# Moving loads, small row transfers and one group of products inside a gated linear attention step that runs ahead of a mixture-of-experts layer

## The chip, the cores and the metric

The kernel runs on one core of a Trainium2 chip. The core has a tensor engine (TensorE, PE in the profile), a vector engine (VectorE, DVE), a scalar engine (ScalarE, ACT), a general engine (GpSimd, POOL) and a sync engine (SyncE, SP) that here only issues transfers. Each engine works through its own instructions in order and waits on semaphores for the others. Transfers are issued from the queues of SP, ACT and POOL and carried by 16 DMA engines. The metric is the device time of one execution in microseconds (us), as the median of several runs. Before the change it is 427.2 us, the median of five runs from 425.12 to 429.56.

## The reference

The reference is a recurrent attention followed by a routed two-layer network. All numbers are 32-bit floats.

```python
batch, n_heads, seq, head_dim = (4, 8, 768, 48)        # q, k, v, alpha
for t in range(S):
    state = alpha[:, :, t, :, None] * state + einsum('bhd,bhe->bhde', k[:, :, t], v[:, :, t])
    y[:, :, t] = einsum('bhd,bhde->bhe', q[:, :, t], state)
x = y.transpose(0, 2, 1, 3).reshape(3072, 384)          # rows for the experts

logits = x @ w_gate                                     # 8 experts
expert_idx = argmax(logits, axis=1)
gate_w = softmax(logits)[row, expert_idx]
for e in range(8):                                      # rows of expert e
    h = maximum(x_sorted[lo:hi] @ w1[e], 0)             # 384 -> 1024
    y_sorted[lo:hi] = h @ w2[e]                         # 1024 -> 384
out = gate_w[:, None] * y_sorted[inv_perm]
```

## The kernel before, in words

**Tiles and steps.** The sequence is cut into 6 chunks of 128 positions. A tile is one chunk of one batch entry, so there are 24 tiles; tile `s` is chunk `s // 4` of batch entry `s % 4`. The attention of a chunk is done in parallel form: alpha's logarithms (`logs`, tile `lna`) are summed along the chunk by one matrix product (`cums`, tile `cum` in one bank of the matrix accumulator, PSUM). The exponential of the sum and of its negative (`cp`, `icp`, on ScalarE) scale q and k (`operands`, tile `kqb`, on GpSimd). Scaled q and k are transposed (`transposes`, `tp`, copied out as `qT` and `kT`), multiplied (`scores`, `sA` and `sB`), masked on VectorE (`mask`, `dA` and `dB`) and multiplied with v (`attend`, into `y`). The state that a chunk inherits from the chunk before is scaled on GpSimd (`scale_state`, tile `U`, needs `acc` of the tile four earlier and the decay `E`) and read with qT (`read_state`, into `y`). `keys_values` and `add_state` build the next state (`acc`). `result` copies y to SBUF (`yT`), and `rows` turns it into rows and router logits by one set of products (tile `x`, one bank). `logits`, `gate` and `gate_weight` finish the router's weight, and `keep_rows` scales the rows (`xs`, ScalarE) and writes them to a table in memory (`x_rows`, SP).

**The order.** One loop over steps `i` from -4 to 23 writes every engine's instructions by hand in the order in which they run. Step `i` does scores, mask, state read and attention of tile `i`, rows of tile `i - 1`, router and `xs` of tile `i - 2`, transposes of tile `i + 1`, operands of tile `i + 2`, and sums some tiles ahead: step 0 takes the sums of tiles 2 and 3, step 1 of 4 and 5, step 2 of 6 and 7, and from step 3 to step 18 it is tile `i + 5`. TensorE's order in a full step is scores, (at the first step of a chunk the transposes `ep` of the decay product), transposes, cum, state read, attention, keys and values, rows. ScalarE's is yT, gex, lna, kT, icp, cp, xs and the issues of the decay rows.

**Decay rows.** What one chunk hands to the next has to be scaled by the end of the chunk before and the start of its own: the last row of `cp` and the first row of `icp` of each tile are moved by small transfers on ScalarE's queue into a tile `dec` per chunk (`decay_out`). Four rows of alpha are loaded beside them on SP's queue (`alpha0`). At the last step of a chunk GpSimd multiplies the three into `er` (`decay_rows`), which the next step transposes into `E` (`decay_cols`).

**Loads.** Pool `ld` holds the loaded tiles of q, k, v and alpha; the loads are issued on SP singly at first and in pairs from step 2. On the same queue stand the writes of `x_rows` and, in steps 4 to 13, ten parts of expert 0's weights (`fetch_part`). Constants for the router (`late_consts`, five parts on GpSimd) are written in steps 1 to 5.

**Experts.** The experts are taken in order of size, each a "place". Place 0 is split: 256 rows (`EARLY`) are gathered and put through both layers around the end of the attention, and what is left, 168 columns in the profile, follows as the rest (`rest_layer1`, `rest_layer2`). The rest's first layer makes eight blocks of 128 hidden units; each is three products into a bank named pB or pC in turn (two buffers of each), and is emptied by ScalarE (even blocks) or VectorE (odd blocks, with pieces of small routing work between, `places`). Its second layer sums over all eight blocks in a bank pA, three times. GpSimd meanwhile gathers rows for the next places by indirect transfers.

Of the kernel before, what the change touches and what calls it, by code (L numbers as in the profile page):

```python
# [8 lines left out]
F32 = mybir.dt.float32  # L9
# [9 lines left out]
def kernel(  # L19
# [29 lines left out]
    nc = tc.nc  # L49
    B, H, S, D = q.shape  # L50
    C = 128
    NB = S // C
    N = B * S
    NT = N // C
    NP = H // 2
# [5 lines left out]
    D2 = 2 * D  # L61
# [69 lines left out]
    def late_consts(i):  # L131
        if i == 0:
            nc.gpsimd.memset(lt_strict[:], 1.0)
            nc.gpsimd.affine_select(
                lt_strict[:], lt_strict[:], compare_op=ALU.is_gt, fill=0.0,
                base=0, pattern=[[1, C]], channel_multiplier=-1,
            )
            nc.gpsimd.memset(ones_sq[:], 1.0)
        if i == 1:
            nc.gpsimd.memset(zero_e[:], 0.0)  # L140
            nc.gpsimd.memset(keep[:], 1.0)
            nc.gpsimd.memset(keep[:, :, 0:1], 0.0)
        if i in (2, 3):
            for ti, tf, pattern, base, mult in list(iotas.values())[4 * (i - 2) : 4 * (i - 1)]:
                nc.gpsimd.iota(ti[:], pattern=pattern, base=base, channel_multiplier=mult)
                nc.gpsimd.tensor_copy(tf[:], ti[:])
            if i == 2:

                nc.gpsimd.memset(key0[:, 0:1], float(16 * N))
        if i == 4:  # L150

            nc.gpsimd.tensor_copy(iota_r[:], iota_f[:])
            nc.gpsimd.tensor_copy(iota_c[:], cols[:])
            tn = tokv[:, NT // 2 :]
            nc.gpsimd.tensor_scalar(tn, tn, scalar1=-float(N + 1), scalar2=None, op0=ALU.add)
# [33 lines left out]
    def fetch_part(g, i):  # L189

        if i == 0:
            g["w1"] = wpool.tile([C, DB, F], F32, name="w1")
            g["w2"] = wpool.tile([C, FB, Dm], F32, name="w2")
        if i < 6:
            a, h = i // 2, i % 2
            nc.sync.dma_start(g["w1"][:, a, h * F // 2 : (h + 1) * F // 2], moe_w1[0, a * C : (a + 1) * C, h * F // 2 : (h + 1) * F // 2])
        else:
            f = 2 * (i - 6)
            nc.sync.dma_start(
                g["w2"][:, f : f + 2], moe_w2[0, f * C : (f + 2) * C, :].rearrange("(a p) d -> p a d", p=C),  # L200
            )
# [161 lines left out]
    with tc.tile_pool(name="ld", bufs=6) as ld, \  # L363
# [32 lines left out]
            nc.scalar.activation(cp[:], cum[:, :Dm], AF.Exp)  # L396
            st[s]["cp"], st[s]["icp"] = cp, icp

        def decay_out(s):
            c, b = cb(s)  # L400
            cp, icp = st[s]["cp"], st[s]["icp"]


            for cc, i, row in ((c, 1, icp[0:1, :]), (c + 1, 0, cp[C - 1 :, :])):
                if 0 < cc < NB:
                    if cc not in decay:
                        decay[cc] = work.tile([B, 2, Dm], F32, name="dec", bufs=3)
                    nc.scalar.dma_start(decay[cc][b : b + 1, i, :], row)
            if b == 0 and c + 1 < NB:
                alpha0[c + 1] = work.tile([B, H, D], F32, name="alpha0", bufs=3)  # L410
                nc.sync.dma_start(alpha0[c + 1][:], alpha[:, :, (c + 1) * C, :])

# [12 lines left out]
        def decay_cols(c):  # L425
            ep = ps.tile([C, NP, C], F32, name="ep", tag="cum")
            for p in range(NP):
                nc.tensor.transpose(ep[:, p, :], pair(er[:], p), ident[:])
            decay[c] = work.tile([C, NP, B], F32, name="E", bufs=2)
            nc.vector.tensor_copy(decay[c][:], ep[:, :, :B])  # L430
# [39 lines left out]
        def scale_state(s):  # L470
            c, b = cb(s)
            if c:
                d = st[s]
                d["U"] = work.tile([C, NP, D], F32, name="U", bufs=3)
                nc.gpsimd.tensor_tensor(
                    d["U"][:], st[s - B]["acc"][:], decay[c][:, :, b].unsqueeze(2).to_broadcast([C, NP, D]), op=ALU.mult,
                )

        def read_state(s):

            if s >= B:
                d = st[s]
                for j in range(2):
                    for p in (2 * j, 2 * j + 1):
                        for g in range(2):
                            o = DP * (p % 2)
                            nc.tensor.matmul(  # L487
                                yv(g)[o : o + D, j, :], lhsT=d["U"][g * DP : g * DP + D, p, :],
                                rhs=d["qT"][g * DP : g * DP + D, p, :], start=(j == 0), stop=False, skip_group_check=True,
                            )  # L490
# [64 lines left out]
        def keep_rows(s):  # L555

            d = st[s]
            xs = work.tile([C, NP, D2], F32, name="xs")
            nc.scalar.activation(xs[:], d["x"][:, :, :D2], AF.Copy, scale=d["gw"][:])  # L559
            nc.sync.dma_start(x_d[s * C : (s + 1) * C, :], xs[:].rearrange("p m d -> p (m d)"))  # L560
            st[s] = {n: t_ for n, t_ in d.items() if n == "acc"}

        def do(f, i, *a):
            if 0 <= i < NT:
                f(i, *a)
# [102 lines left out]
        for i in range(-4, NT):  # L668
            loads_for(i)
            do(scores, i)  # L670
            if i < NT - 1:
                do(result, i - 1)
            do(logits, i - 2)
            if i >= B:
                do(add_state, i - 1)
            do(gate, i - 2)
            if i > 0:
                for s in new_sums(i):
                    logs(s)
            if i == NT - 1:  # L680
                early_turn()
            if 0 < i < NT and i % B == 0:
                decay_cols(i // B)
            do(mask, i, 0)
            do(mask, i, 1)
            if i < B:
                do(add_state, i - 1)
            do(transposes, i + 1)
            sums = list(new_sums(i))
            for s in sums[:1]:  # L690
                cums(s)
            if i < 0:
                for s in sums[1:]:
                    cums(s, "x")
            do(gate_weight, i - 2)
            route(i)
            do(keep_rows, i - 2)
            if i < 0 or len(sums) == 1:
                for s in sums:
                    decay_out(s)  # L700
            if i == NT - 2:
                si = next(se)[1]
                eg["si"] = lambda j, r: si[:r, j : j + 1]
            do(operands, i + 2)
            if i % B == 0:
                do(scale_state, i)
            if 0 < i + 1 < NT and (i + 1) % B == 0:
                decay_rows((i + 1) // B)
            elif i >= 0:
                do(scale_state, i + 1)  # L710
            one_hots(nc.gpsimd, *on_gpsimd.get(i, ()))
            do(read_state, i)
            do(attend, i)
            if i == NT - 2:
                result(i)
            if i >= 0 and sums[1:]:
                cums(sums[1])
                for s in sums:
                    decay_out(s)
            do(keys_values, i)  # L720
            if i == NT - 3:
                held["tok"] = ps.tile([C, NC], F32, name="tok", tag="cum")
                tokens(held["tok"][:], *range((NG - 1) * TG))
                se = early_gather()
            do(rows, i - 1)
            if i in counts_in:
                counts(counts_in[i], counted(i - 1))
            if i < 0:
                for s in new_sums(i + 1):
                    logs(s)  # L730
            if i == -3:
                second_consts()
            late_consts(i - 1)
            if 4 <= i < 14:
                fetch_part(groups[0], i - 4)


        last = NT - 1
# [349 lines left out]
    def rest_layer1(g, beside):  # L1088
        n = g["n"]
        g["h"] = wk.tile([C, FB, CAP0], F32, name="h_sb")  # L1090
        for f in range(FB):
            t = "pB" if f % 2 else "pC"
            hp = mps.tile([C, 512], F32, name=t, tag=t)
            for a in range(DB):
                nc.tensor.matmul(
                    hp[:, :n], lhsT=g["w1"][:, a, f * C : (f + 1) * C], rhs=g["xT"][:, a, :n],
                    start=(a == 0), stop=(a == DB - 1),
                )
            if f % 2:
                nc.vector.tensor_scalar_max(g["h"][:, f, :n], hp[:, :n], 0.0)  # L1100
                next(beside, None)
            else:
                nc.scalar.activation(g["h"][:, f, :n], hp[:, :n], AF.Relu)
# [142 lines left out]
```

## Time and profile before

| Quantity | Value |
|---|---|
| median of 5 runs | 427.2 us (425.12 to 429.56) |
| profiled execution | 424.23 us |
| its span, first to last instruction | 422.5 us |
| mean granted TensorE clock | 0.991 |
| TensorE busy | 406.7 us |
| VectorE busy | 207.9 us |
| ScalarE busy | 171.3 us |
| GpSimd busy | 144.1 us |
| moved by DMA | 59.08 MB, 140 GB/s |

The profile is of one execution. The page gives busy time by engine, the span in 40 slices, the DMA queues, the chain of work that ended last, and the costliest groups of instructions. Further answers of the trace list the instructions of a stretch in order of time: start, duration, engine, line, operation, output and inputs, count, and in square brackets how long the engine stood idle just before and which instruction released it. Lines with ACTq or SPq are issues of transfers from that engine's queue. A table of stretches gives the busy time of every engine in a window, the granted clock (1 is full speed) and the share of the DMA engines' time. A matrix product's end is modelled, so that neighbours overlap a little; the starts are records.

### The profile page before, as it was taken

How to read it: one execution, taken by the hardware profiler on the slowest of the kernel's cores; microseconds unless marked ns; L12 is line 12 of the kernel's file. 1: busy time of each engine (PE TensorE's matmuls, PEld its weight loads, DVE VectorE, ACT ScalarE, POOL GpSimd, SP SyncE). 2: the span in 40 equal slices, each digit the busy share in tenths (PEclk: the TensorE clock that was granted, in tenths of full speed). 3: DMA queues.
4: the chain of work that ended last, by engine and by line, in shares of the span. 5: the costliest groups of instructions: out<-in, count | busy, mean ns of one | idle time of the engine just before them, and what ended most of it. 6: DMA issues, size and time to landing. Idle time of an engine off the chain costs nothing.

```text
span 422.5 us, 9224 instructions
## 1 busy us (share of the span) xinstructions
PE 406.7 (96%) x3525; PEld 343.7 (81%) x3525; DVE 207.9 (49%) x643; ACT 171.3 (41%) x453; POOL 144.1 (34%) x193
## 2 busy tenths in 40 slices
PE   7979999999999999799999999999999999999995
PEld 4658778888888875799879979979979979979952
DVE  5442555464565574264762563563473473453200
ACT  4554656556565430115314513513513523513510
POOL 3438464678668105503201430230240240200101
PEclk9998999999999999989999999999999999999999
DMA  9999899999931219445325154153252352300101
GB/s 176 200 180 228 199 246 210 230 254 211 227 96 39 78 40 320 161 149 175 102 105 170 41 208 162 45 208 100 107 206 77 129 204 72 132 1 2 52 20 35
DMA packets 120099, 59.08 MB, mean 140 GB/s; under 512 B 102935, under 2 KB 114288, under 8 KB 120053
## 3 DMA queue, kind: packets, MB, share of 16 engines
q1 hardware_dynamic: 114932, 48.80, 44.6%
q0 software_dynamic: 3424, 9.59, 6.5%
q8 instruction: 29, 0.48, 0.5%
q10 hardware_dynamic: 1696, 0.08, 0.3%
q14 instruction: 18, 0.14, 0.1%
HBM read 48.95 MB, written 9.58 MB: 139 GB/s over the span
## 4 chain that ended last, share of the span: by engine, by line
PE 80%; issue 6%; DMA 5%; ACT 3%; DVE 1%; SPq 1%; POOL 1%; ACTq 1%; POOLq 0%
PE pA L875 10%; PE pB L875 8%; PE pC L948 8%; PE pA L933 7%; PE y L497 5%; PE sA L460 5%; PE pB L933 4%; PE pC L875 4%; PE tp L447 4%; PE x L534 4%; PE cum L392 3%; DMA x_rows<-xs 2%; PE y L487 2%; PE pC L933 2%; PE tp L791 2%
## 5 line engine op out<-in xcount | busy, mean ns | idle before, releaser
L966 POOL DMA_INDIRECT out_dram<-zo,sp x25 | 27.0, 1082 | 169.6 <-ACT zo L965 118.9
L184 DVE TENSOR_TENSOR h_sb<-pB,u 128x208 f32<-128x208 f32 (+6 forms) x56 | 20.2, 361 | 60.8 <-PE pB L875 43.7
L819 ACT COPY u<-pA 128x208 f32<-128x208 f32 (+6 forms) x68 | 21.7, 319 | 54.0 <-PE pA L933 50.3
L437 POOL TENSOR_TENSOR kqb<-k_sb,icp 128x384 f32<-128x384 f32 x23 | 23.0, 999 | 43.5 <-PE y L508 15.8
L948 PE MATMUL pC<-h_sb,w 128*128 128x416 f32 (+5 forms) x96 | 32.9, 496 | 0.0
L875 PE MATMUL pA<-t,s 128*128 128x208 f32 (+6 forms) x112 | 28.6, 337 | 0.6
L460 PE MATMUL sA<-qT,kT 48*128 48x128 f32 x192 | 27.7, 285 | 0.9 <-ACT kT L453 0.9
L781 POOL DMA_INDIRECT xg<-x_rows,gp x25 | 25.9, 1037 | 7.6 <-issue 6.1
L948 PEld LDWEIGHTS pC<-h_sb,w 128*128 128x128 f32 x96 | 18.1, 190 | 12.0 <-issue 4.4
L460 PE MATMUL sB<-qT,kT 48*128 48x128 f32 x192 | 27.7, 285 | 0.0
L875 PE MATMUL pA<-xgT,w 128*128 128x208 f32 (+6 forms) x112 | 27.7, 329 | 0.0
L447 PE MATMUL tp<-ident,kqb 128*128 128x128 f32 x192 | 26.0, 278 | 0.5 <-DVE kqb L437 0.5
L460 PEld LDWEIGHTS sA<-qT,kT 48*128 48x128 f32 x192 | 23.1, 187 | 4.0 <-ACT kT L453 1.1
L541 DVE TENSOR_REDUCE lgn<-x 128x8 f32<-128x32 f32 x23 | 4.4, 192 | 42.0 <-PE x L534 37.1
L875 PE MATMUL pB<-t,w 128*128 128x208 f32 (+6 forms) x112 | 23.4, 331 | 0.2 <-DVE h_sb L184 0.2
L447 PEld LDWEIGHTS tp<-ident,kqb 128*128 128x128 f32 x192 | 20.8, 140 | 3.3 <-issue 1.0
L437 POOL TENSOR_TENSOR kqb<-q_sb,cp 128x384 f32<-128x384 f32 x23 | 23.0, 1002 | 1.0 <-ACT lna L387 0.6
L888 ACT ACTIVATE h_sb<-h_sb 128x416 f32<-128x416 f32 (+6 forms) x28 | 14.9, 532 | 20.4 <-DVE h_sb L184 20.1
L875 PE MATMUL pC<-xgT,w 128*128 128x208 f32 (+6 forms) x112 | 23.1, 329 | 0.0
L460 PEld LDWEIGHTS sB<-qT,kT 48*128 48x128 f32 x192 | 23.1, 187 | 0.0
L392 PE MATMUL cum<-lna,cum_m 128*128 128x384 f32 x48 | 20.4, 509 | 2.6 <-ACT lna L387 2.5
L534 PE MATMUL x<-iw,yT 128*64 128x104 f32 x368 | 21.6, 261 | 0.8 <-ACT xs L559 0.8
(245 smaller groups left out, 957.5 us busy)
## 6 DMA issues: line engine op xcount, KB each, us to landing
w<-in_moe_w_dram SPq DMA_DIRECT2D x14, 1536.0 KB, 6.5
x_rows<-xs SPq DMA_DIRECT2D x24, 192.0 KB, 3.3
v_sb<-in_v_dram SPq DMA_DIRECT2D x10, 384.0 KB, 5.8
k_sb<-in_k_dram SPq DMA_DIRECT2D x9, 384.0 KB, 6.7
q_sb<-in_q_dram SPq DMA_DIRECT2D x9, 384.0 KB, 5.7
a_sb<-in_alpha_dram SPq DMA_DIRECT2D x8, 384.0 KB, 4.4
a_sb<-in_alpha_dram SPq DMA_DIRECT2D x8, 192.0 KB, 3.9
w<-in_moe_w_dram SPq DMA_DIRECT2D x6, 256.0 KB, 4.4
```

The source lines that it names most:

```text
L392: nc.tensor.matmul(cum[:, :Dm], lhsT=cum_m[:], rhs=st[s]["lna"][:], start=True, stop=True)
L437: eng.tensor_tensor(by_half(kq[:, i]), d[n].rearrange("s (a p) d -> s a p d", a=2), d[e][:].rearrange("s (a p d) -> s a p d", a=2, p=NP), ...
L447: nc.tensor.transpose(tp[:, p, :], pair(kqb[s % 3][:, i], p), ident[:])
L460: nc.tensor.matmul(t[:, p, :], lhsT=d["kT"][r : r + D, p, :], rhs=d["qT"][r : r + D, p, :], start=True, stop=True,)
L497: nc.tensor.matmul(yv(g)[o : o + D, j, :], lhsT=d["v"][:, g * NP + p, :], rhs=d["d" + "AB"[g]][:, p, :], start=(s < B and j == 0), stop=Tr ...
L534: nc.tensor.matmul(d["x"][o : o + HC, m, : D2 + E], lhsT=d["yT"][:, m // 2, m % 2, o : o + HC], rhs=iw[:, m, :], start=True, stop=True,)
L781: nc.gpsimd.indirect_dma_start(out=g["xg"][:r, j, :], out_offset=None, in_=x_d[:, :], in_offset=bass.IndirectOffsetOnAxis(ap=g["gi"](j, r) ...
L819: nc.scalar.copy(t[:, :m], bank["A"][:, :m])
L875: nc.tensor.matmul(out, lhsT=ops[n_][0], rhs=ops[n_][1], start=first and n_ == names[0], stop=True, skip_group_check=True,)
L933: nc.tensor.matmul(out, lhsT=lhs, rhs=rhs, start=first and f == 0, stop=True, skip_group_check=True)
L948: nc.tensor.matmul(d2[:, :n], lhsT=w2[:, f, 2 * C :], rhs=h[:, f, :n], start=(f == 0), stop=(f == FB - 1),)
L966: ins = nc.gpsimd.indirect_dma_start(out=out[:, :], out_offset=bass.IndirectOffsetOnAxis(ap=g["si"](j, r), axis=0), in_=zo[:r], in_offset= ...
```

## The change

- `decay_out` takes an argument that says which of the two rows it moves. In steps 1 and 2 only the `icp` rows of tiles 4 to 7 are moved; their `cp` rows, which chunk 2 needs, follow one by one in steps 3 to 6. The rows of tiles 0 and 1 move from step -2 to step -1, behind the copy of kT, and `alpha0` of chunk 2 moves to step 3 with the `cp` row.
- `xs` has four buffers where it had the pool's two.
- `read_state(i)` is written just ahead of the mask of step `i`, so that on TensorE it stands behind the scores and ahead of the transposes and cum; at the first step of a chunk it stays where it was, behind `scale_state(i)`.
- Parts 0 to 2 of the constants move to step -4, parts 3 and 4 to steps 0 and 1.
- The ten parts of expert 0's weights are asked for in steps 12 to 21.
- The rest's first layer uses banks pC, pB and pA in turn, two buffers each, where it used pC and pB.

```diff
-        def decay_out(s):
+        def decay_out(s, which=(0, 1)):
             c, b = cb(s)
             cp, icp = st[s]["cp"], st[s]["icp"]
-            for cc, i, row in ((c, 1, icp[0:1, :]), (c + 1, 0, cp[C - 1 :, :])):
+            for j in which:
+                cc, row = ((c, icp[0:1, :]), (c + 1, cp[C - 1 :, :]))[j]
                 if 0 < cc < NB:
                     if cc not in decay:
                         decay[cc] = work.tile([B, 2, Dm], F32, name="dec", bufs=3)
-                    nc.scalar.dma_start(decay[cc][b : b + 1, i, :], row)
-            if b == 0 and c + 1 < NB:
+                    nc.scalar.dma_start(decay[cc][b : b + 1, 1 - j, :], row)
+            if b == 0 and c + 1 < NB and 1 in which:
                 alpha0[c + 1] = work.tile([B, H, D], F32, name="alpha0", bufs=3)
...
-            xs = work.tile([C, NP, D2], F32, name="xs")
+            xs = work.tile([C, NP, D2], F32, name="xs", bufs=4)
...
             if 0 < i < NT and i % B == 0:
                 decay_cols(i // B)
+            elif i > 0:
+                read_state(i)
             do(mask, i, 0)
             do(mask, i, 1)
...
-            if i < 0 or len(sums) == 1:
-                for s in sums:
+            if len(sums) == 1:
+                decay_out(sums[0])
+            if i == -1:
+                for s in range(2):
                     decay_out(s)
+
+            if B - 1 <= i < 2 * B - 1:
+                decay_out(i + 1, (1,))
...
-            if i % B == 0:
-                do(scale_state, i)
+            if i > 0 and i % B == 0:
+                scale_state(i)
+                read_state(i)
...
-            do(read_state, i)
             do(attend, i)
...
                 for s in sums:
-                    decay_out(s)
+                    decay_out(s, (0,) if i else (0, 1))
...
-            late_consts(i - 1)
-            if 4 <= i < 14:
-                fetch_part(groups[0], i - 4)
+            if i in (-4, 0, 1):
+                for j in {-4: (0, 1, 2), 0: (3,), 1: (4,)}[i]:
+                    late_consts(j)
+            if 12 <= i < 22:
+                fetch_part(groups[0], i - 12)
...
         for f in range(FB):
-            t = "pB" if f % 2 else "pC"
+            t = "p" + "CBA"[f % 3]
             hp = mps.tile([C, 512], F32, name=t, tag=t)
```

## The prediction

> **What bounds the kernel now.** I read the page's busy shares first, then the table of stretches for the clock and the idle time, then the timelines of TensorE, ScalarE and GpSimd in time order for the places that these point to. Times are us of the profiled span.
>
> ```profile
> PE 406.7 (96%) x3525; PEld 343.7 (81%) x3525; DVE 207.9 (49%) x643; ACT 171.3 (41%) x453; POOL 144.1 (34%) x193
> ```
>
> TensorE is the bound; the other four have half their time free. The stretches tell where it is not:
>
> ```profile
> 20.00:30.00 10.00, 8.62 (x110) 6.34 (x104) 4.37 (x12) 4.70 (x13) 4.20 (x7) 1.00 0.92 180
> 30.00:40.00 10.00, 8.91 (x106) 7.28 (x108) 3.99 (x13) 5.81 (x16) 7.22 (x22) 0.83 1.07 220
> ...
> 90.00:100.00 10.00, 10.00 (x174) 8.07 (x173) 5.28 (x20) 6.20 (x16) 10.00 (x17) 1.00 1.03 239
> ...
> 170.00:180.00 10.00, 7.83 (x50) 7.32 (x49) 3.17 (x16) 1.61 (x5) 5.34 (x6) 0.95 0.41 128
> 180.00:190.00 10.00, 10.00 (x65) 9.79 (x64) 6.77 (x18) 1.67 (x6) 0.00 (x0) 0.88 0.43 157
> ```
>
> Columns: stretch, PE, PEld, DVE, ACT, POOL busy, granted clock, DMA share, GB/s. From 60 to 150 the core is full; it is idle, and twice slow (0.83, 0.88), before 60 and around 175. The TensorE timeline names the waits:
>
> ```profile
> 23.16 0.91 PE L392 MATMUL cum<-lna,cum_m 128*128 128x384 f32 x2 [0.67 <-ACT lna L387]
> ...
> 31.09 0.91 PE L392 MATMUL cum<-lna,cum_m 128*128 128x384 f32 x2 [1.80 <-ACT lna L387]
> ...
> 46.62 0.93 PE L534 MATMUL x<-iw,yT 128*64 128x104 f32 x16 [0.29 <-ACT xs L559]
> ...
> 58.25 0.94 PE L534 MATMUL x<-iw,yT 128*64 128x104 f32 x16 [0.53 <-ACT xs L559]
> ```
>
> Step i is what the loop does for tile i; these four are steps 2, 3, 5 and 7. The first two wait for ScalarE, whose own timeline shows why:
>
> ```profile
> 27.45 0.55 ACTq L408 DMA_DIRECT2D dec<-icp  x1
> 28.09 1.28 ACTq L408 DMA_DIRECT2D dec<-cp  x1
> 29.75 0.59 ACT L516 COPY yT<-y 128x512 f32<-128x512 f32 x1 [2.83 <-DMA dec<-icp]
> ```
>
> Four issues of decay rows, the last held for 1.28, stand ahead of yT, gex and the lna that TensorE needs. Last, a full step (11), TensorE and then ScalarE:
>
> ```profile
> 77.52 1.09 PE L447 MATMUL tp<-ident,kqb 128*128 128x128 f32 x8
> 78.45 0.81 PE L392 MATMUL cum<-lna,cum_m 128*128 128x384 f32 x2
> 79.19 0.66 PE L487 MATMUL y<-qT,U 48*48 48x128 f32 x16
> 79.78 0.64 PE L497 MATMUL y<-dA,v_sb 128*48 128x128 f32 x8
> ...
> 81.04 0.90 PE L534 MATMUL x<-iw,yT 128*64 128x104 f32 x16
> ```
>
> ```profile
> 79.36 0.49 ACT L395 ACTIVATE icp<-cum 128x384 f32<-128x384 f32 x1 [0.56 <-PE cum L392]
> 79.74 0.48 ACT L396 ACTIVATE cp<-cum 128x384 f32<-128x384 f32 x1
> 80.11 0.59 ACT L559 ACTIVATE xs<-x,gw 128x384 f32<-128x384 f32 x1
> ```
>
> cum ends, icp follows within 0.1, then cp, then xs, which ends at 80.70. The x product starts at 81.04 and needs that end, since there is one x bank. The margin is 0.34.
>
> **Part 1, decay rows and expert 0's weights later: the first four steps.** Step 1 loses two and step 2 two of four ACT issues (0.55 each, the held one 1.28). With 1.1 less before yT at 21.82, the lna ahead of cum at 23.16 is done 0.7 before the core asks: the 0.67 goes. In step 2 yT follows the second issue, about 27.4 instead of 29.75, and the 1.80 goes. The clock loss goes with it: in step 3 the stretch from L497 to the next scores took 3.73 (31.93 to 35.66), in step 4 2.10 (39.45 to 41.55), so 1.6. TensorE would reach step 4's state read at 38.87 - 0.67 - 1.80 - 1.6 - 0.1 (kT now ahead of the first two issues) = 34.7.
>
> What is late next is U for that read. GpSimd makes it behind kqb<-q_sb,cp, which ran at 36.74, as soon as its q pair had landed. SyncE issued that pair at 31.38. Ahead of it the v issue at 26.39 took 3.15, against 1.48 to 1.64 for its neighbours of the same size, in the stretch where the DMA engines fall to 1 to 3 tenths (28.8 to 30.0) with ScalarE held too; and an alpha issue of 0.64 (0.75 with its gap) is moved behind. So q comes 1.55 + 0.75 = 2.3 earlier, 34.4; its product 1.0 and U 0.5 end at 35.9. Read at 35.95: gain 2.9, with a new stall of 1.25 in which all of TensorE's queue behind it (attention, keys and values, rows) stands. Ends: 4.2 if q is earlier still; if q lands as before the read starts at 38.2, gain 0.65, and a stall of 3.5 halves the clock again (1.6), a loss of 1.0. I take 2.9, since what holds the two queues at 28 to 29.5 is issued half as often. The decay product er (two of 1.0) comes from rows issued at about 25.9 instead of 27.45, which landed 4.1 later: er ends near 32.1, ep needs it at 32.5, covered by 0.4.
>
> Row against rule: here a gap of 1.80 was followed by a halved clock, and one of 0.67 was not. The Trainium skill's page "TensorE: Matmul & The Clock Gate", section "What's actually happening", puts the cold state after at least one idle window of about 3.4 us, so by the page this gap costs itself alone, and the clock is not there to win: TensorE ready at 36.3, part 1 2.6, part 4 nothing, the sum +0.3, 427.5. The row decides.
>
> The four later cp issues join steps 3 to 6, a third 0.55 behind xs: yT then ends at about 5.45 after the step's transposes began, and acc, which follows it, at 5.9 against the next read at 5.75. I take 0.2 in two steps: +0.4 (0 to 0.6). Their deadline, er of the second chunk at 54.59, is one step (5.45) after the last issue, against a landing of 3.5 to 4.2.
>
> Hidden: the 2.6 of constants on GpSimd fall into its 5.48 idle ahead of 7.73 (if not, kqb of tile 1 is late at once), the others into waits of 2.2 to 2.7. Weights: nothing waits for them before 145.02 (first layer) and 158.22 (second); their last issues now fall near 113 and 135, landing takes 4.4, the DMA share there is 0.16 to 0.33. Each adds 0.42 to SP's queue, behind which x_rows and loads stand that have a step to spare.
>
> **Part 2, four xs tiles.** xs no longer waits for x_rows of two steps before. Without that the products at 46.62 and 58.25 would have started 0.36 after the L508 ahead (45.81, 57.19): 46.17 and 57.55. Gain 0.45 + 0.70 = 1.15; ends 0.8 (idle alone) and 1.2.
>
> **Part 3, state read behind the scores.** In steps that do not begin a chunk, transposes and cum start one read later: 79.78 - 79.19 = 0.59. icp, cp and xs hang on cum back to back, so xs ends at 81.29, and the x product starts 0.04 after that (46.58 to 46.62 above) instead of at 81.04: +0.29. The read itself needs acc (76.84 + 0.36 = 77.20) ahead of 77.52. No gain is there to set against it: these steps have no idle on TensorE. Steps with cum: 5-7, 9-11, 13-15, 17, 18, that is 11 x 0.29 = 3.2. In step 22 xs hangs on kT and qT, ends at 139.67, and 0.59 later would pass the product's start at 139.88 by 0.4. Together +3.6; ends 2.2 (0.2 each) and 4.8 (0.4).
>
> **Part 4, three pairs of banks.** At 175.57 and 178.44 TensorE waits (0.42, 1.75) for banks emptied at 175.21 and 178.06, though their products had ended at 172.6 and 173.4. With six banks all eight blocks finish by 176.8. But layer 2 reads all eight h, and the last is written by DVE at 181.42 to 181.75, behind its small sums. Its first product group then ends near 182.3 instead of 183.52: gain 1.2, less a little for a clock that may fall again. I take 1.0. Ends: 3.4 if the emptying is not late at all (2.17 idle, 1.2 clock), and -0.5 if the idle in front of h turns the clock down for the next group.
>
> **Sum.** -2.9 + 0.4 - 1.15 + 3.6 - 1.0 = -1.05. The profiled execution took 424.23 (span 422.5): 423.2. It lies 3.0 under the median of the five runs, 427.2, so the forecast in that measure is 426.1. Within 0.5% (2.1 us) I call it no change, about what a measurement of this kernel can tell.
>
> **Rivals.**
> Evictions on time: nothing in the rows explains why ScalarE emptied a bank 2.6 after its product; if it doesn't recur, part 4 gives 3.4: -3.45, 423.8. Against it: GpSimd's eight gathers, at the same time, stay.
> The x product doesn't wait: part 3 costs 0.2 at most, sum -4.5, 422.7. It needs xs to start 0.3 sooner after cum, and in every full step the three run back to back.
> Slower: the q pair. It lands at 36.7 as before, GpSimd's queue holds U, TensorE stands 3.5 at step 4's read and the clock halves: part 1 is +1.0, the sum 1.0 + 0.4 - 1.15 + 3.6 - 1.0 = +2.85, 430.0. It decides from a landing of about 36 on, where the stall passes 2.8. For it: the DMA share is 0.92 to 1.13 up to 60. Against: the engines stood idle for 1.2 of that time.
> The change does nothing, loads being the limit throughout: the same as the last, without the clock, +1.2.
>
> **How the numbers follow.** Forecast 0.42, evictions 0.21, no x wait 0.16, q pair 0.17, loads alone 0.04, the last within 0.5%. From these faster 0.37, same 0.46, slower 0.17. The best ends add to -6.6, the worst to +6.1; neither side meets them all together, so the range takes in every case above with a little beyond the fastest: 421.8 to 430.0. The forecast's own range is 424.2 to 428.2.
>
> **What would show it.** Right: no lna wait at cum in steps 2 and 3, clock 1.00 up to 40, a wait of the step-4 read for GpSimd, xs waits of 0.2 to 0.3 at the x product in eleven steps, no wait inside rest's first layer but one ahead of its second. Wrong: steps still 5.45 apart after 60, or a first wait of TensorE for k or q loads.

## The result and the profile after

The changed kernel takes 427.78 us (median of 41 runs, 425.23 to 432.04), the kernel before 424.94 (78 runs, 421.54 to 432.04) beside it. The ratio is 1.007, with a 95% interval of 1.0055 to 1.0086: slower by 0.7%, 2.8 us between the medians. The forecast, no change at 426.1 on a base of 427.2, missed the direction. That 427.78 lies inside the stated range of 421.8 to 430.0 is luck: the five runs of the base lay 2.3 above the 78 measured beside the change, and moved down by that much the range ends at 427.7. The profiled execution took 425.95 us, with a span of 424.2 and a mean granted clock of 0.996 (before: 424.23, 422.5, 0.991).

The table of stretches of the changed kernel (columns as before):

```profile
20.00:30.00 10.00, 9.97 (x126) 7.43 (x124) 5.46 (x16) 7.10 (x19) 4.05 (x5) 1.00 0.97 192
30.00:40.00 10.00, 7.33 (x116) 6.16 (x114) 2.90 (x9) 3.88 (x11) 4.81 (x6) 0.92 1.17 234
90.00:100.00 10.00, 9.76 (x162) 7.79 (x156) 5.68 (x17) 5.60 (x14) 9.86 (x18) 1.00 1.10 214
...
180.00:190.00 10.00, 8.15 (x56) 7.27 (x55) 7.82 (x25) 1.82 (x6) 0.76 (x1) 1.00 0.56 182
```

TensorE is now busy from 20 to 30, as forecast, but it is idle for 2.7 of the next ten, and it is no longer full from 90 to 100, where nothing was to be gained and 0.24 is lost. The hole behind 30 on TensorE's timeline, first the read of before, then the changed kernel:

```profile
38.87 0.65 PE L487 MATMUL y<-qT,U 48*48 48x128 f32 x16
...
33.94 0.81 PE L392 MATMUL cum<-lna,cum_m 128*128 128x384 f32 x2
37.25 0.65 PE L488 MATMUL y<-qT,U 48*48 48x128 f32 x16 [2.50 <-POOL U L476]
37.84 0.65 PE L498 MATMUL y<-dA,v_sb 128*48 128x128 f32 x8
38.31 0.91 PE L498 MATMUL y<-dB,v_sb 128*48 128x128 f32 x8
39.00 0.86 PE L509 MATMUL y<-v_sb,kqb 128*48 128x48 f32 x16
39.65 1.63 PE L535 MATMUL x<-iw,yT 128*64 128x104 f32 x16
```

Both lna waits at cum are gone. TensorE is ready for step 4's read at 34.75 (37.25 - 2.50), where 34.7 was forecast, but the read waits 2.50 for U, and the x product behind it takes 1.63 instead of 0.90: the clock is halved from 38.48 to 41.89. GpSimd and then SyncE in the same stretch, in each block the kernel before above the dots and the changed kernel below:

```profile
36.74 1.01 POOL L437 TENSOR_TENSOR kqb<-q_sb,cp 128x384 f32<-128x384 f32 x1 [0.38 <-ACT gex L548]
37.71 0.52 POOL L475 TENSOR_TENSOR U<-acc,E 128x192 f32<-128x192 f32 x1
...
34.36 1.00 POOL L438 TENSOR_TENSOR kqb<-k_sb,icp 128x384 f32<-128x384 f32 x1 [2.41 <-ACT kT L454]
35.74 0.99 POOL L438 TENSOR_TENSOR kqb<-q_sb,cp 128x384 f32<-128x384 f32 x1 [0.38 <-ACT cp L396]
36.69 0.98 POOL L476 TENSOR_TENSOR U<-acc,E 128x192 f32<-128x192 f32 x2
```

```profile
26.39 3.15 SPq L379 DMA_DIRECT2D v_sb<-in_v_dram  x1
29.64 1.48 SPq L379 DMA_DIRECT2D k_sb<-in_k_dram  x1
31.38 1.62 SPq L379 DMA_DIRECT2D q_sb<-in_q_dram  x1
...
25.79 2.81 SPq L379 DMA_DIRECT2D v_sb<-in_v_dram  x1
28.69 1.44 SPq L379 DMA_DIRECT2D k_sb<-in_k_dram  x1
30.23 1.53 SPq L379 DMA_DIRECT2D q_sb<-in_q_dram  x1
```

The v issue is held for 2.81, hardly less than the 3.15 of before, so the q pair goes out 1.15 earlier and not 2.3, and U, which stands behind its product, starts only 1.0 earlier (36.69 against 37.71). The releaser named at the second product is the cp of a later tile; that of tile 6 was done by 25.77, and the q pair landed at 35.61, 0.13 ahead of the product.

A full step (11) of the changed kernel, TensorE and then ScalarE:

```profile
78.15 0.66 PE L488 MATMUL y<-qT,U 48*48 48x128 f32 x16
78.74 1.09 PE L448 MATMUL tp<-ident,kqb 128*128 128x128 f32 x8
79.67 0.81 PE L392 MATMUL cum<-lna,cum_m 128*128 128x384 f32 x2
...
81.32 0.53 PE L509 MATMUL y<-v_sb,kqb 128*48 128x48 f32 x16
81.97 0.93 PE L535 MATMUL x<-iw,yT 128*64 128x104 f32 x16
```

```profile
80.58 0.49 ACT L395 ACTIVATE icp<-cum 128x384 f32<-128x384 f32 x1 [0.56 <-PE cum L392]
80.96 0.49 ACT L396 ACTIVATE cp<-cum 128x384 f32<-128x384 f32 x1
81.33 0.58 ACT L560 ACTIVATE xs<-x,gw 128x384 f32<-128x384 f32 x1
```

This is as forecast: cum a read later, icp, cp and xs back to back behind it, xs over at 81.91, and the x product at 81.97 instead of 0.36 after 81.32. A step takes 5.77 instead of 5.45.

In the rest, the second layer of place 0 waits in the place of the first (TensorE, the waits of before above the dots, those of the changed kernel below):

```profile
175.57 1.12 PE L1095 MATMUL pC<-xgT,w 128*128 128x168 f32 x6 [0.42 <-issue]
178.44 1.60 PE L1095 MATMUL pB<-xgT,w 128*128 128x168 f32 x6 [1.75 <-issue]
...
180.29 1.16 PE L1121 MATMUL pA<-h_sb,w 128*128 128x168 f32 x7
181.85 0.30 PE L1121 MATMUL pA<-h_sb,w 128*128 128x168 f32 x1 [0.40 <-issue]
183.05 1.12 PE L1121 MATMUL pA<-h_sb,w 128*128 128x168 f32 x6 [0.89 <-ACT h_sb L1113]
184.73 0.55 PE L1121 MATMUL pA<-h_sb,w 128*128 128x168 f32 x2 [0.56 <-DVE h_sb L1110]
```

The balance against the profile of before, by starts: step 4 4.2 ahead (31.48 against 35.66), step 5 0.35 ahead, step 23 3.84 behind (144.53 against 140.69), the turn of place 1 behind the rest 1.76 behind (185.12 against 183.36), and that 1.7 is the difference of the spans.

### The profile page after: what moved, and what is told of

Its sections match the earlier page's. It is cut to its first block, busy times and chain, and to the rows that moved or that the text cites. A ratio compares the mean times of both kernels' runs of the same rounds, so it can differ in the third digit from the quotient of the medians.

```text
span 424.2 us, 9205 instructions
## 1 busy us (share of the span) xinstructions
PE 407.1 (96%) x3525; PEld 342.7 (81%) x3525; DVE 209.0 (49%) x643; ACT 170.4 (40%) x453; POOL 144.0 (34%) x193
## 3 DMA queue, kind: packets, MB, share of 16 engines
HBM read 48.95 MB, written 9.58 MB: 138 GB/s over the span
## 4 chain that ended last, share of the span: by engine, by line
PE 82%; issue 6%; ACT 5%; DVE 2%; DMA 2%; POOL 1%; SPq 1%; ACTq 0%; POOLq 0%; DVEq 0%
PE pA L885 10%; PE pB L885 8%; PE pC L958 8%; PE pA L943 7%; PE sA L461 6%; PE tp L448 5%; PE x L535 5%; PE pB L943 4%; PE pC L885 4%; PE cum L392 3%; PE y L498 3%; PE y L488 3%; PE pA L1093 3%; PE pC L943 2%; PE tp L801 2%
## 5 line engine op out<-in xcount | busy, mean ns | idle before, releaser
L469 DVE TENSOR_TENSOR dA<-sA,cmask 128x512 f32<-128x512 f32 x24 | 16.5, 689 | 12.0 <-PE sB L461 11.9
```

The costliest lines, as they stand in the source:

```text
L469: nc.vector.tensor_tensor(t[:], d["sc"][i][:], cmask[:, None, :].to_broadcast([C, NP, C]), op=ALU.mult)
```

## The experiments

The runs came in three groups, in the order below; each ratio is to runs of the kernel before in the same group (medians 419.45, 423.08 and 420.22). The theory at the start: the read behind the scores costs the time, and step 4's wait for U takes back what part 1 gains. Rivals: the moved transfers cost it, or the loads are the limit.

**The read back in its old place** (the rest as changed):

```diff
-            elif i > 0:
-                read_state(i)
...
-                read_state(i)
...
+            do(read_state, i)
             do(attend, i)
```

> The changed kernel with the state read put back to its old place, behind cum and ahead of attention; everything else stays changed. Theory (the read is what costs): in the changed profile eleven steps take 5.77 where they took 5.45, and step 22 takes 5.66 where it took 4.42, together 11 x 0.32 + 1.24 = 4.8. All of this goes; the x product no longer waits for xs in full steps, they are 5.45 apart again, and the time is 4.8 below the changed kernel, 1.8 below before (ratio 0.996). Rival (the moved transfers cost: weights asked for in steps 12 to 21 and decay rows in steps 3 to 6 lengthen the steps): the steps stay 5.77 apart and the ratio stays near 1.007.

Measured: 0.9946 (0.9924 to 0.9967). Steps are 5.45 apart again, step 22 takes 4.42, and step 23 begins at 138.98 instead of 144.53. Against the changed kernel's 1.007 that is 1.2%, 5.2 us (against its 1.0043 in the third group below, 4.1). The theory holds. The weights asked for in steps 12 to 21 are still there and cost nothing that these steps show.

**The read alone moved, on the kernel before** (the opposite edit):

```diff
+            elif i > 0:
+                read_state(i)
...
+                read_state(i)
...
-            do(read_state, i)
```

> The kernel before with one edit: the state read stands behind the scores in the steps that do not begin a chunk. Theory (the read is what costs): 11 x 0.32 + 1.24 = 4.8 slower, ratio 1.011, with the x product waiting for xs by about 0.3 in full steps and by 1.0 in step 22. Rival (the moved transfers cost): ratio within 0.002 of 1, full steps 5.45 apart.

Measured: 1.0056 (1.0023 to 1.0089), half of what was expected. Full steps take 5.77 and step 22 4.90, so the mechanism is there. But steps 5 to 7 take 17.67 together, against 18.0 with the other parts and 17.56 in the profile of before: xs didn't wait for a write of x_rows in this execution, and the late read stood where such a wait had been; in steps 6 and 13 the read itself waited for acc, 0.28 and 0.48. What the read costs depends on what else is late.

**U ahead of the products of tile 6 in step 4:**

```diff
+            if i == B:
+                scale_state(i)
             do(operands, i + 2)
             if i > 0 and i % B == 0:
-                scale_state(i)
+                if i > B:
+                    scale_state(i)
                 read_state(i)
```

> The changed kernel, but in step 4 GpSimd makes U ahead of the two products of tile 6, so that U no longer stands behind a load. Theory (the queue order at step 4 gives part 1's gain away): E is copied at 33.27, U is done near 34.4, TensorE is ready for the read at 34.75: no wait of 2.50, the clock isn't halved (another 1.7 in steps 4 and 5), and step 5 begins near 37 instead of 41.2; the products of tile 6 end near 36.8, ahead of their transposes at 38. 4.2 below the changed kernel, ratio about 0.997. Rival (loads are the limit up to 60 whatever the order): TensorE waits for k or q of tiles 6 to 9 one or two steps later, the gain is under 1.0, ratio 1.005 or more.

Measured: 1.0021 (0.999 to 1.0052), between the two. Step 4 fell from 9.72 to 6.15 and step 5 began at 37.54; but steps 5 and 6 took 6.49 and 6.98. It wasn't a load. TensorE and then ScalarE of this run:

```profile
36.71 0.90 PE L535 MATMUL x<-iw,yT 128*64 128x104 f32 x16
39.35 0.65 PE L488 MATMUL y<-qT,U 48*48 48x128 f32 x16 [0.65 <-DVE acc L527]
```

```profile
36.36 1.76 ACTq L409 DMA_DIRECT2D dec<-cp  x2
38.16 0.59 ACT L517 COPY yT<-y 128x512 f32<-128x512 f32 x1 [1.80 <-PE x L535]
```

Two held cp issues (the second is part 1's third of the step) stand ahead of yT, acc, at 38.85, waits 0.81 for yT, and the read, which now comes right behind the scores, waits for acc. The two moves meet.

**xs ahead of icp and cp on ScalarE, steps 5 to 18:**

```diff
+            if 5 <= i < 19:
+                do(gate_weight, i - 2)
+                route(i)
+                do(keep_rows, i - 2)
             for s in sums[:1]:
                 cums(s)
...
-            do(gate_weight, i - 2)
-            route(i)
-            do(keep_rows, i - 2)
+            if not 5 <= i < 19:
+                do(gate_weight, i - 2)
+                route(i)
+                do(keep_rows, i - 2)
```

> The changed kernel, but from step 5 to 18 ScalarE makes xs ahead of icp and cp instead of behind them. Theory (the later cum moves icp, cp and xs back to back, and the x product needs the end of xs): xs then ends some 0.9 sooner, before the product is due, full steps are 5.45 apart again although the read stays behind the scores, 11 x 0.32 = 3.5 below the changed kernel, ratio 0.999; step 22 stays at 5.66. Rival (it is the order of TensorE's own queue, or the read's wait for acc): steps stay at 5.77, ratio 1.007.

Measured: 1.0128 (1.0089 to 1.0167). Theory and rival were both wrong about the time. TensorE and then ScalarE in step 14 of this run:

```profile
99.44 0.66 PE L488 MATMUL y<-qT,U 48*48 48x128 f32 x16 [0.57 <-DVE acc L527]
...
102.61 0.53 PE L509 MATMUL y<-v_sb,kqb 128*48 128x48 f32 x16
102.96 0.90 PE L535 MATMUL x<-iw,yT 128*64 128x104 f32 x16
```

```profile
98.25 0.58 ACT L517 COPY yT<-y 128x512 f32<-128x512 f32 x1 [0.85 <-PE x L535]
...
102.14 0.58 ACT L560 ACTIVATE xs<-x,gw 128x384 f32<-128x384 f32 x1 [0.83 <-DVE gw L554]
102.61 0.48 ACT L395 ACTIVATE icp<-cum 128x384 f32<-128x384 f32 x1
102.98 0.49 ACT L396 ACTIVATE cp<-cum 128x384 f32<-128x384 f32 x1
```

The x product's wait for xs did go (102.96 is 0.35 after 102.61), so that wait was what icp and cp ahead of xs had made. But xs now waits 0.83 for gw, which VectorE writes behind the copy of qT, and holds up icp, cp, the issues and yT behind it; the next read then waits for acc, 0.57 in step 14 and 1.92 in step 6. Moving xs forward took away one wait and made others: in this order ScalarE had slack neither at the end of a step nor at its beginning.

**The three pairs of banks alone, on the kernel before:**

```diff
-            t = "pB" if f % 2 else "pC"
+            t = "p" + "CBA"[f % 3]
```

> The kernel before with one edit: the first layer of place 0's rest goes through three pairs of banks instead of two. Theory as predicted: the eight blocks run without a wait, then the second layer waits for the last h; gain 1.0, ratio 0.998. By the changed profile, where the stretch from the rest's first product to the end of its first second-layer group took 11.67 instead of 13.5, the gain is 1.8, ratio 0.996. Rival (evictions on time): no wait ahead of the second layer either, gain 3.4, ratio 0.992.

Measured: 1.0018 (0.9982 to 1.0055): no gain to be seen. The stretch took 11.87, with waits of 0.26, 0.91 and 0.75 ahead of the second layer's products, as in the changed kernel. In the same execution two writes of x_rows were late, in steps 7 and 15, and cost 1.3 and 2.0.

**Part 1 alone, on the kernel before** (all lines of the change on `decay_out`, `late_consts` and `fetch_part`):

```diff
-            late_consts(i - 1)
-            if 4 <= i < 14:
-                fetch_part(groups[0], i - 4)
+            if i in (-4, 0, 1):
...
+            if 12 <= i < 22:
+                fetch_part(groups[0], i - 12)
```

> The kernel before with part 1 alone: decay rows, constants and expert 0's weights later; the read, the xs tiles and the banks as before. Theory (the q pair takes it back): TensorE comes to step 4's read 3 to 4 early and waits there 2 or more for U, which stands behind the product of a q pair that lands near 35.5; steps 5 to 23 begin at most 0.7 earlier than before, ratio 0.998 to 1.000. As predicted: a stall of 1.25, a gain of 2.9 - 0.4 = 2.5, ratio 0.994. If the weights asked for in steps 12 to 21 cost anything, steps 12 to 22 are longer than before (5.45 and 5.88) and the ratio is above 1.

Measured: 0.9972 (0.9944 to 1.0), a gain of about 1.2 with room for none. Step 4 waits 2.12 for U and takes 8.07; the clock was not halved behind it. Steps 12 to 22 are as before, so the weights cost nothing here. Steps 5 to 7 take 18.19, because two writes of x_rows were late in them. The three moves that make up part 1 were not separated.

**Four xs tiles alone, on the kernel before:**

```diff
-            xs = work.tile([C, NP, D2], F32, name="xs")
+            xs = work.tile([C, NP, D2], F32, name="xs", bufs=4)
```

> The kernel before with one edit: four xs tiles. As predicted: the waits of the x product for xs in steps 5 and 7 go, both steps take 5.45 instead of 5.94 and 6.18, gain 1.15, ratio 0.997. Rival (the wait is given back at once, because the writes of x_rows stand in the same queue as the loads): steps 5 to 9 together as long as before, ratio within 0.001 of 1.

Measured: 0.9948 (0.9916 to 0.9979), 2.2 us and twice the forecast. Steps 5 to 7 take 16.34.

**The read back and U first** (the first and the third edit together):

```diff
+            if i == B:
+                scale_state(i)
             do(operands, i + 2)
...
+            do(read_state, i)
             do(attend, i)
```

> The changed kernel with the state read in its old place and, in step 4, U ahead of the two products of tile 6. In the run with U first and the read still behind the scores, step 4 fell from 9.72 to 6.15, but steps 5 and 6 took 6.49 and 6.98 because the read waited for acc, which stood behind yT and held decay row issues of up to 2.2. Theory: with the read in its old place acc is due 2.4 later, the held issues lie beside other work, step 4 takes about 6.1 and steps 5 to 7 about 5.45; 3.4 below the run with the read put back alone, ratio 0.987. Rival (loads are the limit up to 60): steps 5 to 8 stretch until step 9 begins as in the run with the read put back (63.3), ratio 0.994.

Measured: 0.9907 (0.9867 to 0.9946). Step 4 takes 5.88, and step 23 begins at 135.78, 3.2 before the run with the read back alone. Some 1.7 of that is the halved clock behind the wait of that run (37.06 to 40.48), and by the ratios, of different groups, the gain is 1.6. Step 6 takes 6.08: cum waits 0.37 for lna, which stands behind cp issues of 2.25. GpSimd and TensorE of this run:

```profile
33.43 0.52 POOL L476 TENSOR_TENSOR U<-acc,E 128x192 f32<-128x192 f32 x1 [1.24 <-DVE E L431]
33.91 1.01 POOL L438 TENSOR_TENSOR kqb<-k_sb,icp 128x384 f32<-128x384 f32 x1
35.07 1.00 POOL L438 TENSOR_TENSOR kqb<-q_sb,cp 128x384 f32<-128x384 f32 x1 [0.15 <-DMA q_sb<-in_q_dram]
```

```profile
33.85 0.81 PE L392 MATMUL cum<-lna,cum_m 128*128 128x384 f32 x2
34.59 0.66 PE L488 MATMUL y<-qT,U 48*48 48x128 f32 x16
```

No wait is left at the read of step 4, though the product of the q pair still waits for its load. The loads were not the limit there; U's place behind them was.

**The changed kernel with two xs tiles:**

```diff
-            xs = work.tile([C, NP, D2], F32, name="xs", bufs=4)
+            xs = work.tile([C, NP, D2], F32, name="xs")
```

> The changed kernel with part 2 undone: two xs tiles again. Four tiles alone on the kernel before were worth 2.2. Theory (the read behind the scores takes part 2's gain back, because the x product then waits for xs anyway, in steps 5 and 7 as in all others): part 2 is worth under 0.5 in this company, ratio 1.007 to 1.008, steps 5 to 7 within 0.5 of the changed kernel's 18.0. Rival (the parts add): 2.2 slower than the changed kernel, ratio 1.012.

Measured: 1.0045 (1.0012 to 1.0077), against 1.0043 for the changed kernel in the same group. With the read behind the scores part 2 is worth nothing that shows; the intervals reach 1.4 us to either side. Steps 5 to 7 took 19.02, 1.0 and not 0.5 at most above the first profile of the changed kernel (0.7 above the second): the x product waited 0.44 for xs in step 5 and the read 1.11 for acc in step 6, behind cp issues of 1.86. No xs waited more than 0.21 for a write of x_rows.

**The read back, U first, and two pairs of banks:**

```diff
-            t = "p" + "CBA"[f % 3]
+            t = "pB" if f % 2 else "pC"
```

> The kernel with the read in its old place and U first in step 4, but with two pairs of banks in the rest, as before. Theory (three pairs help only when evictions come late, and then the wait moves to the second layer): ratio 0.990 to 0.994, the stretch from the rest's first product to the turn of place 1 between 9.12 (no late eviction) and 13.5. As predicted (part 4 is worth 1.0): 0.993. Rival (the three pairs are worth the 3.4 of all late evictions): 0.999.

Measured: 0.9873 (0.9816 to 0.9931), 415.15 us: faster than both kernels. The rest took 9.12 with two pairs, without a wait. Whether it is better than with three pairs can't be told, since the two ran in different groups.

**Each kernel profiled a second time** (no edit):

> The kernel before, profiled a second time. If the halved clock at 32 and at 179 and the late evictions at 173 to 178 belong to the kernel, they stand in the same places again: steps 3 and 4 take 8.56 and 5.88, the rest 13.5 from its first product to the turn of place 1. If they belong to the execution (where the clock's stretches happen to fall, how late an eviction happens to be), one or more is gone or elsewhere: step 3 near 7.0, the rest between 9.1 and 13.5. Ratio 1.000 either way.

> The changed kernel, profiled a second time. The wait of step 4's read for U (2.50), steps 5.77 apart and step 22's 4.9 to 5.7 belong to the kernel and come again; the halved stretch after the wait and the late evictions in the rest belong to the execution and may not. Ratio 1.007 as measured.

Measured: 0.9966 (0.9927 to 1.0005) and 1.0043 (1.0007 to 1.008). The rest of the kernel before, on TensorE:

```profile
170.34 1.02 PE L1095 MATMUL pC<-xgT,w 128*128 128x168 f32 x6
...
176.33 1.02 PE L1095 MATMUL pB<-xgT,w 128*128 128x168 f32 x6
177.18 2.44 PE L1111 MATMUL pA<-h_sb,w 128*128 128x168 f32 x16
179.46 0.82 PE L791 MATMUL tp<-ident,xg 128*128 128x128 f32 x6
```

With the old two pairs, not one wait: 9.12 instead of 13.5. The xs waits of steps 5 and 7 are gone too (16.33 for steps 5 to 7), and step 11 has one, which the first profile didn't have (ScalarE, then TensorE):

```profile
80.80 0.58 ACT L559 ACTIVATE xs<-x,gw 128x384 f32<-128x384 f32 x1 [1.81 <-DMA x_rows<-xs]
```

```profile
81.43 0.93 PE L534 MATMUL x<-iw,yT 128*64 128x104 f32 x16 [1.46 <-ACT xs L559]
```

The lna wait of 1.78 and the halved clock behind it are there again (32.06). The changed kernel again waits for U (1.56) and has 5.77 in full steps; its clock isn't halved behind the wait, step 22 takes 4.90 and the rest 9.12.

All profiles in one table, in us, from the starts of each step's first score product; "rest" is from its first product to the turn of place 1:

| kernel | step 3 | step 4 | steps 5-7 | step 11 | step 22 | step 23 begins | rest |
|---|---|---|---|---|---|---|---|
| before | 8.55 | 5.89 | 17.56 | 5.44 | 4.42 | 140.69 | 13.50 |
| before, again | 8.48 | 5.90 | 16.33 | 7.11 | 4.43 | 141.12 | 9.12 |
| changed | 5.53 | 9.72 | 18.01 | 5.77 | 5.66 | 144.53 | 11.67 |
| changed, again | 5.23 | 7.74 | 18.33 | 5.77 | 4.90 | 142.12 | 9.12 |
| part 1 alone | 5.61 | 8.07 | 18.19 | 5.45 | 4.44 | 139.67 | 12.89 |
| part 2 alone | 8.21 | 6.17 | 16.34 | 5.44 | 4.42 | 139.19 | 11.69 |
| read alone | 7.29 | 6.07 | 17.67 | 5.77 | 4.90 | 143.16 | 9.12 |
| read back | 5.29 | 9.58 | 16.34 | 5.45 | 4.42 | 138.98 | 9.12 |
| U first | 5.23 | 6.15 | 19.43 | 5.78 | 4.90 | 141.99 | 9.12 |
| read back, U first | 5.23 | 5.88 | 16.97 | 5.44 | 4.43 | 135.78 | 12.75 |
| the same, two pairs | 5.23 | 5.88 | 16.34 | 5.44 | 4.43 | 135.09 | 9.12 |
| xs first | 5.23 | 10.02 | 19.93 | 5.78 | 4.90 | 146.94 | 9.12 |
| banks alone | 6.46 | 7.10 | 17.80 | 5.44 | 4.43 | 142.24 | 11.87 |
| changed, two xs | 5.73 | 8.15 | 19.02 | 5.77 | 4.90 | 143.85 | 9.12 |

## Why the prediction was wrong

**Part 1, forecast -2.9 + 0.4.** The first half was right: with the two lna waits gone, TensorE was ready for step 4's read at 34.8 to 35.1 in the six executions that waited there (forecast 34.7). The step that failed is "I take 2.9, since what holds the two queues at 28 to 29.5 is issued half as often". With half the decay issues, one load issue between 25 and 30 was still held for 2.5 to 3.1 in every run; with all of them it was 2.7 to 3.2. The issues were not what held the queue (what does is not shown). So the q pair moved by 1.15, the wait for U was 1.56 to 2.50 and not 1.25, and the read came at 36.6 to 37.3, not at 35.95. The order named, U behind the q pair in GpSimd's queue, was right, and the runs with U first show it: step 4 took 5.88 and 6.15, where the executions that waited took 7.74 to 10.02. The second failed term is the 1.6 of clock: it was taken from one execution. Of five executions with the old step 3, three lost it; of six with the wait for U, three lost it there. By mean, step 5 begins at 41.03 in the five and at 40.49 in the six, a gain of 0.55; alone, part 1 measured 1.2. That the weights would be hidden came true, though the DMA share near 113 was 0.95 to 1.00 and not the 0.16 to 0.33 that the prediction gives for it.

The +0.4 of the third issue was right in kind (yT, then acc, too late for the read) but held with the read behind the scores, and there it cost more: waits for acc of 0.65 to 1.13 in three of the executions (xs first left aside). They are not the third issue's alone, since the read moved alone had two of 0.28 and 0.48. With the read in its old place and four xs tiles the same three issues cost nothing in two executions (16.34 in steps 5 to 7) and 0.6 in a third, by way of lna (16.97).

**Part 2, forecast -1.15.** Mis-sized, and added where it doesn't add. Alone it was worth 2.2: a late write of x_rows struck in one step or another of each of the four executions with two tiles and the old order that were profiled (steps 5 and 7, in two of them; 11; 7 and 15). They lengthened these steps by 1.2, 1.7, 1.7 and 3.3, and the first profile showed the smallest draw. Beside part 3 it was worth nothing that shows. In the two executions with two tiles and the read behind the scores no xs waited more than 0.21 for such a write, so there was nothing to win in them; why is not shown. That a later xs gives the write time to land is only argued.

**Part 3, forecast +3.6.** The mechanism is right, and 0.29 per step came out as 0.32, step 22's 0.4 as 0.48 in five executions and 1.24 in one (why is not shown). The step that failed is "No gain is there to set against it: these steps have no idle on TensorE": it priced the read against the steps as one profile showed them, alone and added to the other parts alike. Undoing the read in company gave back 5.2 (or 4.1, against 1.0043), alone it cost 2.4. Two things go into the difference as far as the profiles show: the late writes of x_rows that the late read stood in for, and the waits in steps 5 to 7 (18.0 and 18.33 against 16.34, where 3 x 0.29 = 0.9 was counted).

**Part 4, forecast -1.0.** Right in kind: the first layer's waits turn into waits of the second, by up to 0.91, but the size wasn't there. With late evictions and at full clock the stretch took 11.69 and 12.89 with two pairs, 11.67 and 11.87 with three; with a halved clock in it, 13.50 with two and 12.75 with three. That is 0.5 to 0.8 in the mean, and the values overlap. The forecast of 1.0 was sized on the longest of them, and the lateness comes and goes: eight of fourteen executions have none, with two pairs as well as with three, and 9.12 either way. Alone, the part gained nothing to be seen, +0.2% with an interval from -0.2% to +0.6%.

**The rivals.** The "q pair" came closest in time (430.0 on the base of 427.2 is 2.8 slower, as measured) and half in mechanism: U behind the q pair, but the pair 1.15 earlier. The match in time is luck: that rival takes part 1 as a loss of 1.0, where alone it gained 1.2, and counts full gains for parts 2 and 4, which weren't there. Evictions on time came in eight of fourteen executions, of the kernel before too, and were no gain of three pairs. That the x product doesn't wait was wrong in every profile with the read behind the scores and xs in its old place; that loads are the limit in step 4 was refuted by U first.

In sum, the parts that were to give 4.65 (part 1's net 2.5, 1.15 and 1.0) gave 2.3, as the run with the read back shows (0.9946 of 419.45), and the part that was to take 3.6 took 4.1 to 5.2.

## What to carry to other kernels

A wait that one profile shows once or twice, with neighbours of the same kind that don't wait, is a draw: price it by what can be late in any step, and look at a second execution before it enters a sum. When two parts of a change touch the same chain (here cum, icp, cp, xs, the x product on one side and decay issues, yT, acc, the read on the other), cost the second on the schedule that the first leaves; moving work to the front of a step takes the slack of all that has to be done at its front. Where a product stands in a queue behind one that waits for a load, change places before trying to make the load faster: here that gave 1.6 by the ratios (3.2 by step 23 in the profiles, with the clock), on top of part 1, which alone gave 1.2.

## What the runs showed of the hardware

The granted clock fell to half for 3.41 us at a time, and within an execution the starts of these stretches lie on a grid: 32.17 and 178.94 in the first profile are 43.0 x 3.413 apart, 38.08 and 51.73 in the run with xs first are 4.0 x 3.413 apart. The gap's length doesn't decide alone: waits of 1.75, 1.78, 1.79, 1.80, 1.92, 2.04, 2.37 and 2.50 were followed by such a stretch, waits of 1.56, 1.75, 1.83, 1.84, 2.12 and 2.19 were not. Where the gap falls on the grid explains most of it. With the grid laid out from the moment between 4 and 8 us at which the clock first rose to full in each execution, TensorE was idle for 1.78 to 2.37 of the 3.41 us ahead of eight of the nine halved stretches that begin before 410 us, and for at most 1.67 in all other windows from 8 to 410 us but two. These two (1.84 and 1.89, not followed) and the ninth stretch (behind 1.15 in pieces, in the run with the read back and U first) stay unexplained. The Trainium skill's page "TensorE: Matmul & The Clock Gate", section "What's actually happening", says that the window of 3413 ns runs freely and doesn't reset with the kernel, and the grid agrees. It puts the halved state after at least one idle window, and there the measurement differs: windows that were idle for 1.78 to 2.37 of their 3.41 us were enough.

Evictions 1.4 to 5.2 us behind their products, by the products' modelled ends, stood in the rest of both profiles of the result (before and changed) and of all four of the second group. In the first and third groups they came 0.04 to 0.13 behind; the same gathers ran beside them in all. Their cause stays open, and nothing was tried on it. Writes of x_rows held xs up by 0.2 to 2.2 in steps that differ from execution to execution.
